# A front of eight units: priorities, early fillers, shorter conversion and loads from two queues in a 1-core attention and two-layer MoE kernel

## The chip, the cores and the metric

The kernel runs on one core of one Trainium2 chip, in fp32. The metric is the device time of one execution in microseconds. The engines are PE (matmul), DVE (vector), ACT (scalar), POOL (GpSimd) and SP (which issues DMAs).

## The reference

```
for t in range(768):                       # 4 batches x 8 heads, head_dim 40
    y[t]  = r_t . state
    Sa    = state . a_t
    state = state * w_t - Sa (x) b_t + v_t (x) k_t
x = y.transpose(0, 2, 1, 3).reshape(3072, 320)
h = max(x @ w_in, 0);  x = (h * h) @ w_out            # MoE 1, d_ff 2048
g = x @ w_gate;        out = (silu(g) * (x @ w_val)) @ w_out2   # MoE 2, d_ff 1536
```

The weights of both layers arrive as float64, the rest as float32.

## The kernel before

**The recurrence in units.** The 768 steps of all 32 heads are cut into 48 units: unit g holds 32 steps of eight heads and two such sets. Two units make a chain (I), four a block of 256 tokens, and there are 12 blocks. For each unit, e_stage loads `wakb` (w, a, k and b of the unit), takes two scans of products on DVE (L750, L758), a reciprocal (L756), the scaled AB (L754) and two scaled KB products (L762). x_stage multiplies KB with AB on PE (L779), masks the result to L on DVE (L782) and stores a part of L to `xi_d` in DRAM. inverse(w) reads `xi_d` for a window of units (in turn 2, 2, 4, 4, ...), inverts the 16x16 triangular blocks on DVE in 15 pairs of steps (L809, L812), and sends the result to DRAM and back as p1t. beside forms v (L838) and p (L845). chain does what goes from unit to unit: u (L915, L921), s (L934), the Sa tile TV (L944, L945), t (L960), ut (L963), the decayed state ST (L972). slot makes the outputs of one unit: z (L989), c (L998), the masked RC (L1001), y (L1017), yb (L1022), the state copy SX (L1032). k_stage transposes KB (L880). TV holds Sa and the loaded v, so a new chain's v loads (eight each, L705) wait for the last reader of the old one.

**Weights.** [...] The 36 pieces of MoE 1 are converted ahead of and within the first blocks; those of MoE 2 follow between the later blocks and go to DRAM.

**MoE 1.** A block of tokens is written to `xt_d` and read back as `xr`; ACT rounds it to xh (L431), DVE takes the rest as xl (L1051); xh and xl have two buffers. A block is eight pairs P: F, the in-products (L455, 16 matmuls a pair, lines of xh, xl and w1), then gh (ACT) and gl (DVE), then O, the out-products (L460). MoE 2 follows when all blocks are through.

**What sets the order.** A planner (class Plan, L72) writes the instruction order of each engine ahead of time from estimated costs: each operation has a due time (in units), an estimated cost on each engine that may do it, and what it needs; step takes the earliest engine and choose picks among what is ready by due time. On the chip each engine goes through its list in order. fill (L251) puts warm matmuls (L1188) into PE's list where it would idle between the two times of FILL_T (90 and 220 of the planner's us) and no F is ready. A DMA's landing is estimated from its bytes, and each transfer is put behind the one before.

## Time and profile before

| | us |
|---|---|
| median of the runs (lowest, highest) | 1230.94 (1227.38, 1235.12) |
| the profiled execution | 1232.03 |
| its span | 1230.0 |
| PE busy | 1105.3 |
| DVE busy | 677.2 |
| ACT busy | 528.1 |
| POOL busy | 119.3 |
| start of the first in-product (block 0) | 136.90 |
| DVE, mean of one ahead of it: PSUM memset L689, shift L420, w1l L1177 | 0.485, 0.350, 0.445 |
| DVE, the same: reciprocal, L, P, TV, ut, ST, RC, yb | 0.203, 0.417, 0.283, 0.822, 0.484, 0.540, 0.404, 0.423 |
| POOL, memset of 128x1024 | 0.95 |
| PE's one wait for a TV load, 204.4 to 406.7 | 1.6 |

The profiled execution lasted 2.0 us beyond its span and 1.1 us more than the median of the runs. Times inside the span count from its start. "Busy" is the time in which an engine has an instruction, so a difference to the length of a stretch is idle time of that engine.

### The profile page before, as it was taken

How to read it: one execution, taken by the hardware profiler on the slowest of the kernel's cores; microseconds unless marked ns; L12 is line 12 of the kernel's file. 1: busy time of each engine (PE TensorE's matmuls, PEld its weight loads, DVE VectorE, ACT ScalarE, POOL GpSimd, SP SyncE). 2: the span in 40 equal slices, each digit the busy share in tenths (PEclk: the TensorE clock that was granted, in tenths of full speed). 3: DMA queues.
4: the chain of work that ended last, by engine and by line, in shares of the span. 5: the costliest groups of instructions: out<-in, count | busy, mean ns of one | idle time of the engine just before them, and what ended most of it. 6: DMA issues, size and time to landing. Idle time of an engine off the chain costs nothing.

```text
span 1230.0 us, 44840 instructions
## 1 busy us (share of the span) xinstructions
PE 1105.3 (90%) x19570; PEld 1048.1 (85%) x19570; DVE 677.2 (55%) x1645; ACT 528.1 (43%) x1216; POOL 119.3 (10%) x146
## 2 busy tenths in 40 slices
...
GB/s 163 125 155 121 150 124 168 172 171 101 170 166 167 152 163 113 106 101 105 99 105 80 77 72 50 110 116 117 12 11 25 25 16 21 25 25 25 12 12 14
DMA packets 171093, 115.08 MB, mean 94 GB/s; under 512 B 104168, under 2 KB 147368, under 8 KB 170888
## 3 DMA queue, kind: packets, MB, share of 16 engines
...
q14 instruction: 50, 0.41, 0.1%
...
## 4 chain that ended last, share of the span: by engine, by line
PE 68%; DVE 10%; DMA 9%; issue 5%; SPq 4%; ACT 3%; POOL 1%; DVEq 0%; POOLq 0%; ACTq 0%
PE ps L455 32%; PE ps L460 20%; SPq L705 3%; PE ps L1017 2%; DMA ws<-f_moe_w_val 2%; DMA TV<-in_v_t_dram 2%; PE ps L921 2%; DMA wakb<-in_wakb_dram 2%; PE ps L998 2%; PE ps L989 1%; PE ps L934 1%; DMA room<-xt_d 1%; PE ps L779 1%; DVE qt L812 1%; PE ps L915 1%
## 5 line engine op out<-in xcount | busy, mean ns | idle before, releaser
L1361 DVE TENSOR_TENSOR gr<-ps,gr 128x512 f32<-128x512 f32 x144 | 99.5, 691 | 174.5 <-ACT gr L1358 161.0
L1099 ACT ACTIVATE ps<-ps 128x512 f32<-128x512 f32 x192 | 112.0, 584 | 118.4 <-PE ps L455 115.8
L460 PE MATMUL ps<-o1h,gh 128*128 128x320 f32 x384 | 132.9, 346 | 4.6 <-ACT gh L431 3.7
L460 PE MATMUL ps<-o1h,gl 128*128 128x320 f32 x384 | 122.8, 320 | 2.3 <-DVE gl L406 2.2
L460 PE MATMUL ps<-o1l,gh 128*128 128x320 f32 x384 | 121.3, 316 | 0.0
L455 PE MATMUL ps<-xh,w1h 128*128 128x256 f32 x384 | 119.0, 310 | 0.3 <-issue 0.3
L455 PE MATMUL ps<-xl,w1h 128*128 128x256 f32 x384 | 111.5, 290 | 3.9 <-DVE xl L1051 2.6
L455 PE MATMUL ps<-xh,w1l 128*128 128x256 f32 x384 | 111.0, 289 | 0.0
L1358 ACT ACTIVATE gr<-ps 128x512 f32<-128x512 f32 x72 | 43.2, 600 | 157.6 <-PE ps L455 156.0
L406 DVE TENSOR_TENSOR gl<-ps,gh 128x512 fp32r<-128x512 f32 x96 | 65.7, 685 | 63.0 <-ACT gh L431 62.7
L431 ACT CAST gh<-gr 128x512 fp32r<-128x512 f32 x72 | 44.7, 620 | 112.5 <-DVE gr L1361 106.5
L460 PE MATMUL ps<-o2h,gh 128*128 128x320 f32 x288 | 89.0, 309 | 2.0 <-ACT gh L431 2.0
L460 PE MATMUL ps<-o2h,gl 128*128 128x320 f32 x288 | 88.9, 309 | 0.2 <-DVE gl L1083 0.2
L460 PE MATMUL ps<-o2l,gh 128*128 128x320 f32 x288 | 88.8, 308 | 0.0
L460 PEld LDWEIGHTS ps<-o1h,gh 128*128 128x128 f32 x384 | 74.3, 194 | 8.9 <-ACT gh L431 5.3
L455 PE MATMUL ps<-xh,wgh 128*128 128x256 f32 x288 | 81.3, 282 | 0.2 <-DVE gr L1361 0.2
L455 PE MATMUL ps<-xl,wgh 128*128 128x256 f32 x288 | 80.2, 279 | 0.2 <-DVE xl L406 0.2
L455 PEld LDWEIGHTS ps<-xl,w1h 128*128 128x128 f32 x384 | 75.9, 198 | 5.0 <-DVE xl L1051 3.1
L455 PE MATMUL ps<-xh,wgl 128*128 128x256 f32 x288 | 79.9, 277 | 0.0
L455 PE MATMUL ps<-xh,wvh 128*128 128x256 f32 x288 | 79.7, 277 | 0.0
L455 PE MATMUL ps<-xl,wvh 128*128 128x256 f32 x288 | 79.7, 277 | 0.0
L455 PE MATMUL ps<-xh,wvl 128*128 128x256 f32 x288 | 79.6, 276 | 0.0
(161 smaller groups left out, 3035.3 us busy)
## 6 DMA issues: line engine op xcount, KB each, us to landing
...
```

Of the source, the lines that this page charges most:

```text
L406: nc.vector.tensor_sub(dst, full, hi.bitcast(F32))
L431: nc.scalar.copy(dst, src) if e == ACT else eng[e].tensor_copy(dst, src)
L455: nc.tensor.matmul(ps, w[:, c], x, start=(i == 0), stop=(i == len(seq_) - 1))
L460: nc.tensor.matmul(acc[t][:, :DM], g[:, half, ts], w[:, f, :], start=(f == 0 and i == 0), stop=(f == nf - 1 and i == 2),)
L705: return att({SP: slow or 0.42}, lambda e: nc.sync.dma_start(dst(), src()), r, w, due=due, dma=dma, tag="dma")
L779: nc.tensor.matmul(v[64 * p:64 * p + 64, jh, u], kb[:, s, :], ab[:, s], start=True, stop=True)
L921: nc.tensor.matmul(quad(tag)[64 * p:64 * p + 64, u, n], AB[nas[u]][:, s].rearrange("e q t -> e (q t)"), ST[u][:, s, 0:D], start=False, sto ...
L998: nc.tensor.matmul(v[64 * p:64 * p + 64, jh, u], RW[:, 4 * jh + 2 * u + p], RB[:, :, s], start=True, stop=True)
L1017: nc.tensor.matmul(v[64 * q:64 * q + D, p, s], w, x, start=not kb, stop=bool(kb))
L1099: op({ACT: 0.478}, lambda e, f=f: nc.scalar.activation(P1[b], P1[b], f), (), (("p", b),), due=due, tag="relu")
L1358: op({ACT: 0.478}, lambda e: nc.scalar.activation(two["gr"][n], two["pg"][b], AF.Sigmoid), (("pg", b),), (("gr", n),), tag="sig", **kw)
L1361: op({DVE: 0.602}, lambda e, q=q: nc.vector.tensor_mul(two["gr"][n], two[q][b], two["gr"][n]), ((q, b),), (("gr", n),), tag="u" + q, **kw)
```

## The change

Each of these is one edit; all of them act on what the planner orders or on what is computed around it.

- front(i) takes 12 units off the due times of units 0 to 3 and 6 off those of units 4 to 7. The first window is four units.
- `wakb` of units 0 to 3 comes in two pieces; eight units in place of four may use the two buffers that lie in `room`.
- The v and r loads (TV, RB, RH) of the first eight units may be issued by ACT or SP.
- BACKLOG: a load that waits for no data is issued when what is queued lasts no more than 1.2 us by the planner's estimate; the estimates of `wakb`, RB and the weight pieces are lower.
- TV and RW have two buffers. xh and xl have one in MoE 1: high_low of the next block is put in the order behind the last pair of a block; MoE 2 has two of its own.
- conv_ops: five operations. Copy with a scale of 2^-112 takes the place of Abs, the max goes, the masks follow.
- The two KB products are one of twice the elements, on DVE alone. Clears of POOL and the PSUM clears of DVE are copies from a blank tile on ACT, but for two on POOL and the blank tile's on DVE.
- FILL_T starts at 3 in place of 90. The first five weight pieces have due -9; the others come into the list behind unit 7's e_stage.

```
+        o.bulk = bool(cost) and SP in cost and not r
...
+        if o.bulk:
+            t = max(t, self.dma - BACKLOG)
...
-        t = self.free[PE]
+        t = max(self.free[PE], now - 0.02)
...
-        if t < FILL_T[0] or t > FILL_T[1] or any(o.cols for o in ok) or self.moe_cols(t + d - self.TICK, t + d) >= RAMP[2]:
+        if t < FILL_T[0] or t > FILL_T[1] or any(o.cols or t < FILL_T[2] for o in ok) or self.moe_cols(t + d - self.TICK, t + d) >= RAMP[2]:
...
+BACKLOG = 1.2
+SIDE = 4
+HEAD = 4
+AHEAD_DUE = 12.0
+W1_FIRST = 5, -9.0
...
-WIN0 = 2, 2
+WIN0 = 4,
...
-INIT_DUE = -1.0, -2.0
-HURRY = 0, 0, 0, 3
...
-FILL_T = 90.0, 220.0
+FILL_T = 3.0, 220.0, 3.0
...
-            ({ACT: t_act(n)}, lambda e: nc.scalar.activation(t.bitcast(F32), hi_f, AF.Abs), "x", "t"),
-            ({DVE: t_dve2(n), POOL: t_pool(n)}, lambda e: eng[e].tensor_scalar(
-                out=t.bitcast(F32), in0=t.bitcast(F32), scalar1=F64_TINY, scalar2=None, op0=ALU.max), "t", "t"),
+            ({ACT: t_act(n)}, lambda e: nc.scalar.activation(t.bitcast(F32), hi_f, AF.Copy, scale=F64_BASE), "x", "t"),
             ({DVE: t_dve2(n)}, lambda e: nc.vector.tensor_scalar(
-                out=t, in0=t, scalar1=3, scalar2=0x3FFFFFF8, op0=ALU.logical_shift_left, op1=ALU.bitwise_and),
+                out=t, in0=t, scalar1=3, scalar2=0x7FFFFFF8, op0=ALU.logical_shift_left, op1=ALU.bitwise_and),
                 "t", "t"),
             ({DVE: t_dve(n)}, lambda e: nc.vector.scalar_tensor_tensor(
-                out=t, in0=hi_i, scalar=-0x40000000, in1=t, op0=ALU.bitwise_and, op1=ALU.bitwise_or), "xt", "t"),
+                out=t, in0=hi_i, scalar=-0x80000000, in1=t, op0=ALU.bitwise_and, op1=ALU.bitwise_or), "xt", "t"),
...
-    xhs = ring(mp, 2, [128, 3, BT], F32R, "xh")
-    xls = ring(mp, 2, [128, 3, BT], F32R, "xl")
+    xhs = ring(mp, 1, [128, 3, BT], F32R, "xh")
+    xls = ring(mp, 1, [128, 3, BT], F32R, "xl")
...
-    TV = ap_.tile([128, 2, 8, 64], F32, name="TV")
+    TVS = ring(ap_, 2, [128, 2, 8, 64], F32, "TV")
...
-    RW = ap_.tile([EPAD, 8, 2 * C], F32, name="RW")
+    RWS = ring(ap_, 2, [EPAD, 8, 2 * C], F32, "RW")
...
+    blank = TVS[1].rearrange("p u m d -> p (u m d)")
+    nc.vector.memset(blank, 0.0)
     for b in range(8):
-        nc.vector.memset(PS[32:64, b], 0.0)
+        nc.scalar.copy(PS[32:64, b], blank[32:64, 0:512])
...
+        return -AHEAD_DUE if i < HEAD else -AHEAD_DUE / 2 if i < 2 * HEAD else 0.0
...
+    queues = {SP: nc.sync, ACT: nc.scalar}
+
+    def load(dst, src, r, w, due, dma, slow=0.0, both=False):
+        cost = {SP: slow or 0.42}
+        if both:
+            cost[ACT] = cost[SP]
+        o = att(cost, lambda e: queues[e].dma_start(dst(), src()), r, w, due=due, dma=dma, tag="dma")
+        o.bulk = not r
+        return o
 
...
-        due = g - LA + E_DUE
+        due = g - LA + E_DUE + front(g)
...
-        load(lambda: WA[wa(g)], lambda: a["wakb"][data(g)], (), (kw, ka0, ka1, kk), due - 1, 2.4)
+        if g < HEAD:
+            load(lambda: WA[wa(g)][:, 0:NWA], lambda: a["wakb"][data(g)][:, 0:NWA], (), (kw,), due - 1, 0.5)
+            load(lambda: WA[wa(g)][:, NWA:], lambda: a["wakb"][data(g)][:, NWA:], (), (ka0, ka1, kk), due - 1, 1.35)
+        else:
+            load(lambda: WA[wa(g)], lambda: a["wakb"][data(g)], (), (kw, ka0, ka1, kk), due - 1, 1.8)
...
-        for k, n in ((0, 2), (1, 1)):
-            att(two, lambda e, k=k, n=n: eng[e].tensor_mul(
-                kb[:, :, k * C:(k + 1) * C], akb[:, n], rd),
-                (kw, kk), (("KB", nk),), due=due + 0.3, tag="km", port=True)
+        att({DVE: t_dve(16 * C)}, lambda e: nc.vector.tensor_mul(
+            kb.rearrange("p s (k t) -> p k s t", k=2), akb[:, 2:0:-1], rd[:, None].to_broadcast([EPAD, 2, 8, C])),
...
-        early = FIRST if w == 0 else 0.0
+        n, due = 2 * ns * H, q0 - INV_DUE + front(q0)
...
+        if e == POOL:
+            att({POOL: t_pool(n) / 2}, lambda e: nc.gpsimd.memset(v, 0.0), (), ks, due=due, tag="init")
+        else:
+            att({ACT: t_act(n)}, lambda e: nc.scalar.copy(v, blank[0:t.shape[0], 0:n]), kblank, ks, due=due, tag="init")
...
-                         lambda p=p, jh=jh, vsrc=vsrc: vsrc[p, jh], (), (("Tv", u, p, jh),), due - 0.7, 0.12, 0.62)
+                         lambda p=p, jh=jh, vsrc=vsrc: vsrc[p, jh], (), (("Tv", b, u, p, jh),), due - 0.7, 0.12, 0.62, I < SIDE)
...
-        load(lambda: RB.rearrange("p q s t -> p (q s t)"), lambda: a["vr_e"][data(i)][:, 1], (), ("Rv",), due - 0.3, 1.2)
...
+        load(lambda: RB.rearrange("p q s t -> p (q s t)"), lambda: a["vr_e"][data(i)][:, 1], (), ("Rv",), due - 0.3, 0.9, 0.0, i < 2 * SIDE)
...
+    def high_low(blk):
+            due, kr = to_x[blk]
+            xh, xl, kx = xhs[0], xls[0], ("xh", 0)
...
+        if p == NP1 - 1 and blk + 1 < NBLK:
+            high_low(blk + 1)
...
-           kxs + [names["l"]], due=due - 1, dma=n * 1024 / 180e3, tag="dW")
+           kxs + [names["l"]], due=due - 1, dma=n * 1024 / 240e3, tag="dW")
...
-    for k, job in enumerate(w1):
-        conv(job, W1_DUE[0] + W1_DUE[1] * k / len(w1), False)
...
+            if q == 2 * HEAD - 1:
+                op(None, lambda: None, (), [("wa", x, n) for x in range(4) for n in (2, 3)] + [("xr", k) for k in range(3)]
+                   + [("o", n) for n in range(2)] + [("cx", NCX - 1), ("cl", NCX - 1)])
+                for k, job in enumerate(w1):
+                    conv(job, W1_FIRST[1] if k < W1_FIRST[0] else W1_DUE[0] + W1_DUE[1] * k / len(w1), False)
+        if I == 2:
...
+        if I == 2:
+            high_low(0)
...
+        two["xh"] = ring(sp2, 2, [128, 3, BT], F32R, "xh2")
+        two["xl"] = ring(sp2, 2, [128, 3, BT], F32R, "xl2")
```

**PE from the first chain's u.** L915 and L921 of before are L953 and L959 of after, L779 is L801 (x), L838 is L860 (v), L845 is L867 (p), L1188 is L1236 (a filler). Before:

```order
L779 MATMUL ps<-AB_148,KB_134 64x64 x8
L779 MATMUL ps<-AB_149,KB_135 64x64 x8
L915 MATMUL ps<-TV,L_123 32x40 x16
L915 MATMUL ps<-TV,L_124 32x40 x16
L921 MATMUL ps<-ST_153,AB_146 64x40 x8
L921 MATMUL ps<-ST_154,AB_147 64x40 x8
L779 MATMUL ps<-AB_150,KB_136 64x64 x8
L779 MATMUL ps<-AB_151,KB_137 64x64 x8
L779 MATMUL ps<-AB_152,KB_132 64x64 x8
L838 MATMUL ps<-p1t,L_123 32x16 x16
```

and after:

```order
L801 MATMUL ps<-AB_146,KB_132 64x64 x8
L1236 MATMUL ps<-warm 128x256 x16
L801 MATMUL ps<-AB_147,KB_133 64x64 x8
L953 MATMUL ps<-TV_157,L_121 32x40 x16
L953 MATMUL ps<-TV_157,L_122 32x40 x16
L959 MATMUL ps<-ST_151,AB_144 64x40 x8
L959 MATMUL ps<-ST_152,AB_145 64x40 x8
L1236 MATMUL ps<-warm 128x256 x90
L801 MATMUL ps<-AB_148,KB_134 64x64 x8
L1236 MATMUL ps<-warm 128x256 x2
L860 MATMUL ps<-p1t,L_121 32x16 x16
L860 MATMUL ps<-p1t,L_122 32x16 x16
```

Behind the first chain's u stand 90 fillers, then the x product of one more unit, and only then v, which waits for the first inverse; before, three x products stand there and no filler.

**SP between the first `wakb` loads and the first read of `xi`.** `pt_d` is a table of zeros in DRAM, cx a weight piece, `xi_d` the stored part of L. Before:

```order
L705 DMA RH<-in_r_e_dram 40x512 x2
L705 DMA TV<-in_v_t_dram 32x4x40 x8
L705 DMA wakb_166<-in_wakb_dram 104x1040
L705 DMA xi_d_60<-L_123 32x256 x2
L705 DMA wakb_167<-in_wakb_dram 104x1040
L705 DMA xi_d_60<-L_124 32x256 x2
L705 DMA xi_d_61<-L_125 32x256 x2
L705 DMA xi_d_61<-L_126 32x256 x2
L1147 DMA room<-in_moe_w_out_dram 128x320
L1147 DMA cx_116<-in_moe_w_out_dram 128x320
L1147 DMA cx_117<-in_moe_w_in_dram 128x256
L705 DMA xi<-xi_d_60 32x16x16 x2
```

and after:

```order
L722 DMA xi_d_60<-L_121 32x256 x2
L722 DMA TV_157<-in_v_t_dram 32x4x40 x4
L722 DMA xi_d_60<-L_122 32x256 x2
L722 DMA RB<-in_vr_e_dram 104x512
L722 DMA xi_d_60<-L_123 32x256 x2
L722 DMA RH<-in_r_e_dram 40x512
L722 DMA TV_158<-in_v_t_dram 32x4x40 x4
L722 DMA xi_d_60<-L_124 32x256 x2
L1195 DMA cx_114<-in_moe_w_in_dram 128x256
L1195 DMA cx_115<-in_moe_w_in_dram 128x256
L1195 DMA cx_116<-in_moe_w_in_dram 128x1x256
L722 DMA xi<-xi_d_60 64x16x16 x2
```

The stores to `xi_d` of four units in place of two stand ahead of the read of `xi`; eight v loads stand between them, the other eight of the first two chains are in ACT's list, and no further `wakb` load stands ahead of the read.

**ACT around the first xh.** L416 and L417 (after: L422, L423) open a conversion, L713 (after: L732) are sums of squares for a range test at the end. Before:

```order
L431 CAST o1h<-ct_120 128x320
L416 ACTIVATE room<-room 128x256
L417 ACTIVATE ct_122<-room 128x256
L431 COPY KT_157<-ps 128x320
L431 CAST w1h_99<-ct_121 128x256
L713 ACTIVATE sq,stat<-DT_142 104x256
L431 CAST w1h_100<-ct_122 128x256
L431 CAST xh_111<-room 128x768
L713 ACTIVATE sq,stat<-wakb_166 104x256
```

and after:

```order
L422 ACTIVATE room<-room 128x320
L423 ACTIVATE ct_120<-room 128x320
L435 CAST o1h<-ct_120 128x320
L732 ACTIVATE sq,stat<-wakb_167 104x256
L435 CAST w1h_99<-ct_118 128x256
L732 ACTIVATE sq,stat<-DT_138 104x256
L435 CAST w1h_100<-ct_119 128x256
L435 CAST o1h<-ct_117 128x320
L435 CAST xh_111<-room 128x768
L435 COPY vt<-ps 128x8x16
```

The xh of block 0 stands behind the same kinds of work in both; of the weight pieces, 22 are loaded ahead of the first pair before, and 13 after.

## Rows read from the trace of the kernel before

**Rows 1.** The first part of the page: busy us, share of the span, instructions

```profile
PE 1105.3 (90%) x19570; PEld 1048.1 (85%) x19570; DVE 677.2 (55%) x1645; ACT 528.1 (43%) x1216; POOL 119.3 (10%) x146
```

**Rows 2.** Windows, cut at block starts: length, PE, PEld, DVE, ACT, POOL, granted clock, DMA share

```profile
0.00:97.00 97.00, 44.70 (x1088) 38.16 (x1089) 83.26 (x251) 38.91 (x114) 29.10 (x44) 1.00 0.55 143
0.00:136.90 136.90, 74.17 (x1945) 64.38 (x1946) 108.35 (x309) 53.45 (x157) 35.83 (x52) 0.96 0.54 141
136.90:204.40 67.50, 55.33 (x1301) 50.69 (x1300) 50.40 (x133) 42.58 (x108) 21.16 (x24) 0.90 0.55 143
204.40:272.20 67.80, 59.81 (x1310) 55.36 (x1309) 45.04 (x126) 37.16 (x88) 14.46 (x16) 0.93 0.67 184
272.20:346.00 73.80, 63.27 (x1586) 57.88 (x1586) 48.63 (x132) 38.15 (x95) 13.49 (x14) 0.96 0.48 126
346.00:406.70 60.70, 56.53 (x1249) 52.80 (x1249) 39.37 (x109) 33.38 (x81) 9.73 (x11) 0.90 0.60 161
```

**Rows 3.** Timeline around block 0's first in-product: start, us, engine, line, operation

```profile
133.88 0.83 ACT L431 CAST xh<-room 128x768 fp32r<-128x768 f32 x1
...
134.74 0.96 DVE L1051 SCALAR_TENSOR_TENSOR xl<-room,xh 128x768 fp32r<-128x768 f32 x1 [0.31 <-ACT xh L431]
...
136.90 0.41 PE L455 MATMUL ps<-xh,w1h 128*128 128x256 f32 x1
```

**Rows 4.** PE's waits, 0 to 136.9: us in total, times, longest us

```profile
PE ps L779 <- DVE KB L762: 36.8, 7, 16.0
```

**Rows 5.** DVE's groups, 0 to 136.9: busy us, mean ns, idle time ahead

```profile
L809 DVE TENSOR_TENSOR tmp<-qt,xi 64x15 f32<-64x15 f32 (+15 forms) x45 | 10.8, 240 | 2.1 <-DMA xi<-xi_d 1.2
L762 DVE TENSOR_TENSOR KB<-wakb 104x256 f32<-104x256 f32 x22 | 10.2, 477 | 0.2
L754 DVE TENSOR_TENSOR AB<-wakb,DT 40x256 f32<-40x256 f32 x20 | 10.1, 507 | 0.2
L812 DVE TENSOR_TENSOR qt<-qt,tmp 64x15 f32<-64x15 f32 (+15 forms) x45 | 9.6, 213 | 1.1
...
L423 DVE SCALAR_TENSOR_TENSOR ct<-cx,ct 128x256 int32<-128x256 int32 (+1 forms) x15 | 7.1, 477 | 0.0
...
L418 DVE TENSOR_SCALAR ct<-ct 128x256 f32<-128x256 f32 (+1 forms) x17 | 5.5, 326 | 0.4 <-ACT ct L417 0.4
...
L1177 DVE TENSOR_TENSOR o1l<-ct,o1h 128x320 fp32r<-128x320 f32 x7 | 4.5, 650 | 0.3 <-ACT o1h L431 0.2
```

**Rows 6.** Timeline of SP's queue

```profile
13.76 9.69 SPq L705 DMA_DIRECT2D TV<-in_v_t_dram  x8
```

**Rows 7.** The chain of waits, pieces up to block 0: start, us, what

```profile
23.57 4.41 DMA wakb<-in_wakb_dram
...
138.97 2.92 DMA xi<-xi_d
```

**Rows 8.** Timeline of PE: two x products

```profile
52.55 1.12 PE L779 MATMUL ps<-AB,KB 104*64 104x64 f32 x16 [16.02 <-DVE KB L762]
...
107.33 0.69 PE L779 MATMUL ps<-AB,KB 104*64 104x64 f32 x16
```

**Rows 9.** Timeline: POOL and DVE side by side, at two places

```profile
7.16 0.36 POOL L902 MEMSET SX<- 104x320 f32 x1
7.16 0.71 DVE L750 TENSOR_TENSOR_SCAN DT<-wakb,c 104x264 f32<-104x264 f32 x1 [1.46 <-DMA wakb<-in_wakb_dram]
...
39.25 0.91 POOL L425 TENSOR_TENSOR ct<-ct,room 128x320 int32<-128x320 int32 x1 [1.82 <-DVE tmp L809]
39.35 0.83 DVE L812 TENSOR_TENSOR qt<-qt,tmp 64x15 f32<-64x15 f32 x1
```

**Rows 10.** PE's waits, 204.4 to 406.7

```profile
PE ps L845 <- ACT ct L417: 3.5, 1, 3.5
...
PE ps L455 <- DVE xl L1051: 2.6, 2, 2.2
```

**Rows 11.** The chain of waits of the whole span, one out-product

```profile
850.86 3.52 PE ps L460 x24
```

115 lines of the change are left out of this document (62 added, 53 removed).

## The prediction

> **What bounds the kernel now.** The page's first part comes first: PE is busy for 1105.3 of 1230.0 us [rows 1], so the time is PE's work plus what PE loses, and the question is where it loses. The table of windows, cut at the first F matmul of each token block (the end of the front, 136.90, is the first L455 in the timeline [rows 3]), shows where: in the front, 0 to 136.9, PE is busy for 74.17 us, fillers included, so 62.7 are idle; the next four blocks lose 12.2, 8.0, 10.5 and 4.2; what lies behind runs at 90% or more and holds PE work that the change leaves alone [rows 2]. So the change is worth what it shortens the front, less the work that it pushes out of it, plus what it does to the next four blocks.
>
> What sets the front? DVE is busy for 108.35 of its 136.9 us, for 83.26 of the first 97 [rows 2], and the chain of waits to 138.29 is mostly DVE rows with pieces of SP and DMA between. PE's own waits there are one line in the main: its x products wait for DVE's KB 36.8 us in 7 waits [rows 4], which is PE standing in order behind a late DVE. So I count DVE operations.
>
> **The front, part by part.** The count is of DVE instructions ahead of the first xl in each order; each goes by its mean in the front [rows 5].
> - conv_ops without the max step, and fewer jobs ahead of block 0: max 17 to 0 (17 x 0.326 = 5.5), shift 20 to 12 (8 x 0.350 = 2.8), L423 20 to 12 (8 x 0.477 = 3.8), the w1l/o1l subtractions 15 to 8 (7 x 0.54, between 445 and 650, = 3.8). Sum 15.9.
> - The inverse of one four-unit window in place of two of two units: 90 operations to 60. They cost 240 and 213 ns, so 30 x 0.227 = 6.8. A tile of 128 rows in place of 64 costs the same here, since the elements of a row stay.
> - Fewer units ahead of block 0: scans 26 to 22 (4 x 0.71 = 2.8), AB 24 to 16 (8 x 0.507 = 4.1), and one each or so of L, P, TV, ut, ST, RC, yb and reciprocals (5.1).
> - KB: 26 products of 0.477 (the four of `room` 0.402) are 11.7 us; 11 merged ones of twice the elements take their place. No row has one. Bounds: 0.69, on the line between the 256 elements of w1l (0.445) and the 768 of xl (0.96 [rows 3]), and 0.95, twice 0.477. I take 0.75, since xl, the only row with more elements, is as wide as the merged product in partitions and lies far under three times 0.477: 8.3 us, 3.4 less.
> - Clears: eight PSUM memsets of 0.485 leave DVE for ACT; one memset of 128x1024 comes (the same shape cost POOL 0.95), 2.9 less. ACT takes some 16 copies, about 8 us, in its empty start (38.91 busy of 97 [rows 2]), at no price while DVE waits for its first wakb, until 7.16 [rows 9]; up to 2 if the split load lets the first scan start earlier and a clear stands before it.
>
> Sum 40.9: DVE's work falls from 108.35 to 67.4 us. The loads of v and r: eight TV issues hold SP for 9.69 us from 13.76 [rows 6], while DVE waits for the `wakb` behind them (23.57, 4.41 on the chain [rows 7]). In the order of after some of them stand on ACT, so two queues share the 1.2 us a piece.
>
> DVE's idle time in the front was 136.9 - 108.35 = 28.55. I keep two thirds, 19 us, as the waits for the first wakb (7) stay, and the waits from TV issues fall. A new wait comes: the first inverse needs the L of all four units, and the store of the fourth stands on SP behind four TV issues (4 x 1.21 = 4.8); then `xi` has to land (2.92 [rows 7]): 8 us in which DVE has little ready, since the conversion is ordered behind. So 27 idle, and block 0 starts at 67.4 + 27 = 94 us, bounds 78 (idle 11, as if the new wait is covered and SP no longer shows) to 105 (idle 38: the new wait doubles). That is 43 us earlier. But PE has done 12 groups fewer by then: at 0.69 each, the x row at 107.33 [rows 8], 8.3 us that come later. Net 34.6.
>
> **Early fillers.** Fillers grow from 80 to 308 matmuls, 244 of them ahead of block 0, in idle time of PE. They raise the clock if anything: 16 x products took 1.12 us at 52.55 behind a 16 us gap and 0.69 at 107.33 [rows 8]. Yet the table's granted clock reads 1.00, the 2.4 GHz level, over 0 to 97 [rows 2], and the front hangs on DVE; a group on the chain saves 0.4, and with some eight on it, 3 us. I book nothing, as a filler ahead of a late group delays it by about as much as it saves.
>
> **The port.** At 39.25 a POOL addition of 0.91 us stands beside a DVE step of 0.83 that takes 0.213 in the mean, while a POOL memset at 7.16 leaves the scan beside it at 0.71, its usual time [rows 5, 9]. So clears that go to ACT give DVE nothing beyond its own eight. Eight L425 additions fewer ahead of block 0 (they fall with the jobs) may free 8 x 0.6 = 5 us; I book nothing, since a mean of 213 over 45 steps says that such meetings are few.
>
> **Blocks 0 to 1.** The work that left the front comes here. DVE's count between the first and second xl is 20.2 us higher (no max, but 11 more shifts, 10 more L423, 6 more wl, four scans, and so on by the same means): 50.40 + 20.2 = 70.6. How full DVE can run decides: in the front's first 97 us it was busy 0.86 of the time (83.26/97), here 0.75 (50.40/67.5), in the next three 0.65 to 0.66 [rows 2]. I take 0.86, since here, as in the front and unlike in the stage before, there would be more DVE work than PE work: 82 us against 67.5, 14.5 more, which holds the 13 us of PE work (17 groups and a u) that moved in. Net loss 1.5; at 0.75 it would be 94 us, 12 worse, at 0.65 109, 27 worse. The sum stands at 33.
>
> **Blocks 1 to 4.** Before, PE was idle for 12.2 + 8.0 + 10.5 + 4.2 = 35 us in blocks 0 to 3 [rows 2]; its waits from 204 to 407 are many small ones, by name L845 for a conversion's ct 3.5 and F for xl 2.6 [rows 10], for a TV load 1.6. Two Sa buffers take the TV wait away, a max less per job shortens the ct wait, fewer conversions wait on DVE: 8 of 35 us, bounds 0 and 20. Behind 406.7 nothing is moved that PE waits for: two `xh` in MoE2 as before.
>
> **The single xh/xl buffer** adds a wait: xh of the next block may not be written before the last F of this one, and xl behind it holds up the next F: 0.83 + 0.96 [rows 3]. PE then has 12 L460 matmuls (half of 24 in 3.52 [rows 11], 1.76) and one group each of c, x and z (three at 0.69 [rows 8]): 3.8 us that cover 1.8 and two hand-overs. I book zero; what is queued in order behind them on ACT and DVE is conversions, due later.
>
> **Sum.** 34.6 - 1.5 + 8 = 41 off 1232.0, the profiled execution's own time, is 1191; it lies 1.1 above the median of the runs, so 1190. From the bounds: 78 in the front with 20 in the blocks gives 1162; 105 and no gain in the blocks, 1209; the rivals reach to 1222.
>
> **Rivals.**
> 1. *Conversion takes the gain back* (0.18). ACT and DVE run in order; jobs that were ahead of block 0 now interleave with e-stage and F's gh/gl. For it: DVE's share was 0.65 in three of four blocks [rows 2]. Against: there PE was the busier. The stage is 27 longer: 1232 - 41 + 27 - 1 = 1217.
> 2. *DMA binds* (0.11). Block 0 needs 13.4 MB by the order of after; at 141 GB/s [rows 2] that is 95 us, already the forecast. If the rate stays there because the transfers and not the issues limit it, and the short queue (BACKLOG) lets the engines run dry for a tenth of the time, block 0 comes 11 us later, and so does block 1 by as much again (12.8 MB): 1232 - 41 + 23 - 1 = 1213. Against: DMA's share is 0.55 there and rose to 0.67 at 184 GB/s in a later block [rows 2], so there is room. The Trainium skill speaks for this rival ("DMA: Bandwidth & Descriptors", section "Issuing engines are not separate DMA queues"): transfers that another engine starts run on the same 16 DMA engines, and a second issuer saves no more than the time of the issue. The 9.69 us that eight issues take are such time, so the trace leaves the rule standing and the gain too.
> 3. *Slower* (0.07): the one xh/xl. Each of 11 block starts waits with ACT and DVE in order: if a gh, a conversion pair and an e-stage piece stand ahead of xh, 5 us are lost beyond the cover, 55 in all: 1232 - 41 + 55 - 1 = 1245. It decides from (41 + 12)/11 = 4.8 us each. Against: blocks started before with xl as the last to come [rows 3, 10] and lost 2.6 in two waits.
> 4. *More* (0.12): block 0 at 80, blocks 1 to 4 losing 15 in place of 35: 1164.
> That the change doesn't do what it says is open only for fillers and port, which I booked at nothing.
>
> **How the numbers follow.** The forecast, 1190, has 0.52; the rivals the rest. The range of 1160 to 1222 holds all but rival 3 and some of rival 1's tail. A measurement of this kernel tells 1% from no change: 12.3 us, so faster is under 1218.6 and slower over 1243. Faster: 0.52 + 0.11 + 0.12 + 0.10 of rival 1 = 0.85; same 0.08, from rival 1's; slower 0.07.
>
> **What would show it.** In the profile of after: first L459 at 94 (78 to 105); DVE about 67 us busy ahead of it; second block's first F 82 us behind; merged KB at 0.75; PE's longest wait in the front the one for the first inverse, at 25 to 35 us; no wait for TV in blocks 1 to 4; waits of F for xl under 1 us a block. I am wrong if block 0 starts past 105, if block 0 takes 100 or more, or if xl waits come to 5 a block.

## The result, and the profile after

The kernel after takes 1224.39 us in the median of 20 runs (1211.89 to 1237.83), the kernel before 1234.38 (1224.03 to 1241.7): a ratio of 0.9911, interval 0.9885 to 0.9936. The ratio goes by the executions in the faster of the chip's two states, 18 of the 20 of after. It is faster, by 0.9% or 11 us, where 41 were forecast; 1190 and the range up to 1222 are both missed on the high side. By the forecast's own line of 12.3 us for telling a change this counts as the same, to which it gave 0.08; the interval excludes no change all the same. Before itself measures 3.4 us more here than the 1230.94 under the forecast: on that base 0.9911 is 1220, inside the range at its upper end. So the range is missed by less than two measurements of before differ, but of the gain only a quarter came.

The profiled execution of after lasted 1218.24 us (span 1216.3), 6 less than its median, so the sums below, against the 1232.03 of before, come to 13.8 and not to 11.

The first part of the page of after, to be read against [rows 1]:

```profile
PE 1128.3 (93%) x19798; PEld 1072.6 (88%) x19798; DVE 643.4 (53%) x1492; ACT 538.4 (44%) x1238; POOL 106.3 (9%) x127
```

PE's span that is not busy falls from 124.7 to 88.0 us, yet PE is busy for 23.0 us more. The windows of after, cut at the first F of blocks 0, 1, 4 and 11 (columns as in [rows 2]):

```profile
0.00:111.00 111.00, 72.99 (x1724) 65.53 (x1725) 73.09 (x192) 49.94 (x134) 20.33 (x30) 0.86 0.52 133
111.00:214.00 103.00, 83.78 (x2031) 76.45 (x2029) 70.21 (x173) 62.13 (x161) 36.41 (x38) 0.85 0.54 149
214.00:388.40 174.40, 166.81 (x4033) 154.63 (x4029) 115.19 (x305) 95.65 (x234) 22.89 (x26) 0.96 0.57 149
388.40:760.80 372.40, 361.69 (x8555) 336.01 (x8553) 199.48 (x529) 192.06 (x442) 25.88 (x32) 0.99 0.45 116
760.80:1216.30 455.50, 443.04 (x3468) 439.95 (x3466) 185.48 (x296) 138.59 (x269) 0.74 (x1) 0.99 0.13 35
```

And before, from its block 0 on, cut at its first F of blocks 1 (205.4; [rows 2] cut it at 204.4), 4 and 11:

```profile
136.90:205.40 68.50, 56.33 (x1318) 51.41 (x1317) 50.99 (x134) 42.58 (x108) 21.16 (x24) 0.90 0.55 143
205.40:406.70 201.30, 178.61 (x4128) 165.32 (x4126) 132.45 (x363) 108.69 (x264) 37.67 (x40) 0.93 0.58 156
406.70:784.90 378.20, 365.12 (x8720) 339.19 (x8721) 200.57 (x544) 185.10 (x419) 23.86 (x29) 0.99 0.41 102
784.90:1230.00 445.10, 431.08 (x3467) 427.84 (x3465) 184.80 (x296) 138.27 (x269) 0.74 (x1) 0.99 0.13 35
```

Fillers alone take 15.7 us before, all in the front; after, PE's fillers in the front and in block 0:

```profile
0.00:111.00 111.00, 40.48 (x244) 0.86 0.52 133
111.00:214.00 103.00, 10.65 (x66) 0.85 0.54 149
```

| stage, us | before | after | measured | forecast | PE's own work | idle and fillers |
|---|---|---|---|---|---|---|
| front | 136.9 | 111.0 | -25.9 | -43 | -26.0 | +0.1 |
| block 0 | 68.5 | 103.0 | +34.5 | +14.5 | +16.8 | +17.7 |
| blocks 1 to 3 | 201.3 | 174.4 | -26.9 | -12.7 | -11.8 | -15.1 |
| blocks 4 to 10 | 378.2 | 372.4 | -5.8 | 0 | -3.4 | -2.4 |
| block 11 and MoE 2 | 445.1 | 455.5 | +10.4 | 0 | +12.0 | -1.6 |

The forecast column follows from the sum on record: what it moves into block 0, and the part of that which comes from later blocks, stands with the stage in which it is saved or paid. The last two columns split the measured change: PE's own work is its busy time without fillers, the rest of a stage is idle time and fillers. The first three stages moved in the direction given; the two booked at nothing gain 5.8 and lose 10.4.

**The front.** DVE's groups in the front of after (busy us, mean ns, idle time ahead):

```profile
L831 DVE TENSOR_TENSOR tmp<-qt,xi 128x15 f32<-128x15 f32 (+7 forms) x30 | 6.7, 225 | 6.6 <-DMA xi<-xi_d 5.8
...
L773 DVE TENSOR_TENSOR_SCAN DT<-wakb,c 104x264 f32<-104x264 f32 x7 | 5.7, 810 | 2.2 <-DMA wakb<-in_wakb_dram 2.2
...
L784 DVE TENSOR_TENSOR KB<-wakb 104x512 f32<-104x512 f32 x7 | 5.4, 773 | 0.0
...
L424 DVE TENSOR_SCALAR ct<-ct 128x256 int32<-128x256 int32 (+1 forms) x12 | 4.9, 404 | 10.7 <-ACT ct L423 10.5
...
L784 DVE TENSOR_TENSOR KB<-room 104x512 f32<-104x512 f32 x4 | 2.7, 669 | 0.0
```

The merged KB takes 0.773 and 0.669 us, 0.735 in the mean, so 0.75 was a good guess, and a step of the inverse costs 225 ns on 128 rows where it cost 240 on 64 [rows 5]. Single rows moved (this scan from 0.71 [rows 9] to 0.810, the shift from 0.350 to 0.404, the inverse's steps down), but the durations of DVE's operations ahead of block 0 add up to 121.4 us before and 80.3 after, 41.1 less, as counted (40.9). DVE's busy time falls by 35.3 only, to 73.1 us and not 67.4: in the record the spans of neighbouring operations overlap, by 13 us in all before and 7 after, and the forecast took durations off a busy time. And DVE idles 37.9 us and not 27, of which 10.5 are for the ct that ACT makes (L423) and 5.8 for `xi`. Both lie in one place, as DVE's timeline shows (start, duration, engine, line; the idle time ahead in brackets), and SP's under it:

```profile
19.11 0.42 DVE L804 TENSOR_TENSOR L<-ps,mask 128x256 f32<-128x256 f32 x1 [1.32 <-PE ps L801]
28.43 0.29 DVE L424 TENSOR_SCALAR ct<-ct 128x256 int32<-128x256 int32 x1 [8.89 <-ACT ct L423]
...
35.00 0.17 DVE L831 TENSOR_TENSOR tmp<-qt,xi 128x15 f32<-128x15 f32 x1 [5.82 <-DMA xi<-xi_d]
```

```profile
19.77 3.03 SPq L722 DMA_DIRECT2D TV<-in_v_t_dram  x4
22.89 0.99 SPq L722 DMA_DIRECT2D xi_d<-L  x2
23.93 2.56 SPq L1195 DMA_DIRECT2D cx<-in_moe_w_in_dram  x3
26.60 4.05 SPq L722 DMA_DIRECT2D xi<-xi_d  x2
```

The last L of the first window ends at 19.53. Its stores stand behind four TV issues, as foreseen (19.77, 3.03 long); then SP issues three weight pieces for 2.56 us, and then the reads of `xi`, 4.05 us long. The inverse begins at 35.00: in 15.5 us DVE does two conversion steps. The term was 8.

**PE's waits.** Two rows, one of the front, one of 214 to 388 (in total, times, longest):

```profile
PE ps L801 <- DVE KB L784: 17.1, 2, 15.9
...
PE ps L459 <- DVE xl L1097: 0.2, 1, 0.2
```

The 36.8 us of [rows 4] fell to 17.1, and the single xh/xl costs nothing: F waits for xl 0.2 us in three blocks, as booked. No wait names a TV load there. PE's longest wait in the front, 15.9 us, ends at 48.35 and is for a KB; the forecast had expected one for the first inverse at 25 to 35.

### The profile page after: what moved, and what is told of

It reads as the page before. It is cut to its first block, busy times and chain, and to the rows that moved or that the text cites. A ratio compares the mean times of both kernels' runs of the same rounds, so it can differ in the third digit from the quotient of the medians.

```text
span 1216.3 us, 45103 instructions
## 1 busy us (share of the span) xinstructions
PE 1128.3 (93%) x19798; PEld 1072.6 (88%) x19798; DVE 643.4 (53%) x1492; ACT 538.4 (44%) x1238; POOL 106.3 (9%) x127
## 3 DMA queue, kind: packets, MB, share of 16 engines
q1 hardware_dynamic: 168462, 110.58, 34.6%
## 4 chain that ended last, share of the span: by engine, by line
PE 70%; DMA 5%; SPq 3%; DVE 3%; issue 2%; ACT 2%; DVEq 0%; ACTq 0%
PE ps L459 33%; PE ps L464 22%; SPq L722 3%; PE ps L1056 2%; DMA ws<-f_moe_w_val 2%; PE ps L1037 2%; PE ps L1028 1%; PE ps L959 1%; PE ps L998 1%; PE ps L1071 1%; DMA P<-pt_d 1%; PE ps L801 1%; PE ps L972 1%; PE ps L867 1%; PE ps L953 1%
## 5 line engine op out<-in xcount | busy, mean ns | idle before, releaser
L459 PE MATMUL ps<-xh,w1h 128*128 128x256 f32 x384 | 116.0, 302 | 0.2 <-issue 0.2
L435 ACT CAST gh<-gr 128x512 fp32r<-128x512 f32 x72 | 44.6, 620 | 112.0 <-DVE gr L1410 106.2
L412 DVE TENSOR_TENSOR gl<-ps,gh 128x512 fp32r<-128x512 f32 x96 | 65.5, 682 | 43.6 <-ACT gh L435 43.4
L464 PEld LDWEIGHTS ps<-o1h,gl 128*128 128x128 f32 x384 | 74.6, 194 | 5.3 <-DVE gl L412 5.3
```

Source lines behind the costliest of these rows:

```text
L412: nc.vector.tensor_sub(dst, full, hi.bitcast(F32))
L435: nc.scalar.copy(dst, src) if e == ACT else eng[e].tensor_copy(dst, src)
L459: nc.tensor.matmul(ps, w[:, c], x, start=(i == 0), stop=(i == len(seq_) - 1))
L464: nc.tensor.matmul(acc[t][:, :DM], g[:, half, ts], w[:, f, :], start=(f == 0 and i == 0), stop=(f == nf - 1 and i == 2),)
```

## Experiments

**What had to be told apart.** The forecast had one frame: the time is PE's work plus its idle time, so the kernel gains what the front loses. Four readings of the miss stood against each other: that the conversion of MoE 1's weights, pushed out of the front, filled block 0; that early fillers stand in PE's way; that MoE 2, whose x tiles got another place, works more slowly; and that the planned order scatters so much that small terms mean nothing. Words in capitals in the expectations are names of such readings. All ratios are to the kernel before; in the table are also the starts of three blocks (their first F) and the length from block 11 on, from each run's profile. Before has 205.4, 784.9 and 445.1 for the last three columns.

| run | ratio | interval | block 0 | block 1 | block 11 | last stage |
|---|---|---|---|---|---|---|
| after | 0.9911 | 0.9885-0.9936 | 111.0 | 214.0 | 760.8 | 455.5 |
| after_again | 0.9898 | 0.9842-0.9953 | 113.5 | 215.9 | 766.9 | 455.5 |
| jit_x | 0.992 | 0.9879-0.996 | 111.0 | 209.3 | 769.0 | 457.0 |
| jit_add | 0.9913 | 0.9876-0.9951 | 110.9 | 208.5 | 773.6 | 457.5 |
| x2_high | 0.98 | 0.9765-0.9835 | 110.0 | 212.5 | 770.3 | 447.9 |
| late_fill | 0.9835 | 0.9794-0.9876 | 113.7 | 199.7 | 756.3 | 457.3 |
| x2_late | 0.9768 | 0.9721-0.9816 | 116.5 | 198.7 | 752.5 | 445.8 |
| split_late | 0.9787 | 0.9712-0.9863 | 114.1 | 198.7 | 752.5 | 451.2 |
| no_prio | 0.9915 | 0.9876-0.9954 | 124.4 | 188.2 | 771.1 | 456.6 |
| max_back | 0.9926 | 0.9884-0.9967 | 116.5 | 221.9 | 774.2 | 455.2 |
| w1_earlier | 0.9988 | 0.9951-1.0024 | 108.5 | 197.9 | 775.8 | 455.0 |
| xi_gate | 0.9951 | 0.9917-0.9985 | 117.7 | 208.8 | 773.9 | 455.6 |
| one_queue | 1.0008 | 0.9979-1.0038 | 110.7 | 197.4 | 775.2 | 456.1 |
| long_queue | 1.0006 | 0.9966-1.0046 | 114.1 | 199.2 | 786.1 | 456.2 |
| x2l_one | 0.9864 | 0.9807-0.9921 | 110.7 | 213.7 | 767.8 | 447.8 |
| x2l_long | 0.9974 | 0.994-1.0008 | 129.7 | 194.9 | 784.8 | 447.0 |
| x2l_short | 1.0385 | 1.031-1.0461 | 103.8 | 196.6 | 824.0 | 458.3 |

Two more ran only once: w1_cheap (1209.51 us) and x2_mixed (1208.18).

### The place of MoE 2's x tiles: x2_high, x2_mixed, split_late

After takes MoE 2's two xh and two xl from the ring at the low end of the partition. x2_high lays the odd blocks' tiles into the pool of the out-weights at the high end, and lets the even ones use MoE 1's. MoE 2's weights, which lie behind that ring, move back down with it; the order of DVE's and ACT's operations is that of after.

```
-        two["xh"] = ring(sp2, 2, [128, 3, BT], F32R, "xh2")
-        two["xl"] = ring(sp2, 2, [128, 3, BT], F32R, "xl2")
...
+        two["xh"] = [xhs[0]] + ring(wo2, 1, [128, 3, BT], F32R, "xh2")
+        two["xl"] = [xls[0]] + ring(wo2, 1, [128, 3, BT], F32R, "xl2")
```

> One edit to the changed kernel: MoE 2's two xh and two xl no longer lie beside MoE 2's input weights but at the far end of the partition (one pair is MoE 1's tile, the other a new one behind o2), as far from the weights as in the kernel before. The order up to block 11 stays. Theory PLACE: in the changed kernel MoE 2's in-products start 120 ns apart where they were 113 ns apart before, because the moved operand now lies in the same part of SBUF as the weights; here the spacing is 113 to 114 again, the last stage (block 11's first in-product to the end) takes 445 in place of 455.5 us, the run about 11 us less than the changed kernel (near 1213). Rival RUN: the 120 is a state of that run or follows from something else in the program (the order, the new weight offsets); then the spacing stays at 119 to 120 and the time at about 1224.

The step of the blocks of MoE 2 is read from the timeline of DVE's xl (L406 before, L412 after), here two successive blocks of before, of after and of x2_high:

```profile
1013.71 1.02 DVE L406 TENSOR_TENSOR xl<-ps,xh 128x384 fp32r<-128x384 f32 x2
...
1046.90 1.02 DVE L406 TENSOR_TENSOR xl<-ps,xh 128x384 fp32r<-128x384 f32 x2
```

```profile
1028.08 1.02 DVE L412 TENSOR_TENSOR xl<-ps,xh 128x384 fp32r<-128x384 f32 x2
...
1062.26 1.02 DVE L412 TENSOR_TENSOR xl<-ps,xh 128x384 fp32r<-128x384 f32 x2
```

```profile
1034.65 1.02 DVE L412 TENSOR_TENSOR xl<-ps,xh 128x384 fp32r<-128x384 f32 x2
...
1067.98 1.02 DVE L412 TENSOR_TENSOR xl<-ps,xh 128x384 fp32r<-128x384 f32 x2
```

The step is 33.19, 34.18 and 33.33 us. And inside a block, by PE's timeline, successive in-products of before and of after:

```profile
999.73 0.28 PE L455 MATMUL ps<-xh,wvl 128*128 128x256 f32 x1
999.85 0.28 PE L455 MATMUL ps<-xh,wvhl 128*128 128x256 f32 x1
999.96 0.28 PE L455 MATMUL ps<-xl,wvhl 128*128 128x256 f32 x1
```

```profile
1000.06 0.28 PE L459 MATMUL ps<-xh,wvh 128*128 128x256 f32 x1
1000.18 0.28 PE L459 MATMUL ps<-xl,wvh 128*128 128x256 f32 x1
1000.30 0.28 PE L459 MATMUL ps<-xh,wvl 128*128 128x256 f32 x1
```

Every product lasts 0.28, but they start 113 ns apart before and 120 after: same shapes, same clock (0.99 in both windows), no wait between. In x2_high the last stage is 447.9 in place of 455.5 and the ratio 0.98 against 0.9911 (0.9898 in the second measurement): the place costs about 1%. The last stage shows 7.6 us of it, 0.6%; the intervals leave room for that.

x2_mixed keeps the xl of odd blocks at the low end, beside the weights, and moves the rest as x2_high does.

> As the run with MoE 2's x far away, but the xl of odd blocks stays beside the weights, all else far. PLACE, and the operand is what counts: in-products that read xh, and those of even blocks that read xl, start 113 ns apart; those of odd blocks that read xl 120, all within one execution. If the offset of the weights counts and not that of x, all are equal. If one near tile disturbs the others, odd blocks are slow throughout.

Its last stage is 450.4, between the two; the products of xh and of xl are 118 and 120 ns apart in its odd blocks, 113 in its even ones: the third reading, odd blocks slow throughout, and with the weights in one place, so that the place of x matters by itself. split_late is x2_late (below) with MoE 1's x and g tiles in a pool of their own at the start of the partition:

```
+    xg = xgs.enter_context(tc.tile_pool(name="xg", bufs=1, side="left"))
...
-    xhs = ring(mp, 1, [128, 3, BT], F32R, "xh")
+    xhs = ring(xg, 1, [128, 3, BT], F32R, "xh")
```

> The kernel with late fillers and MoE 2's x far from its weights, and one edit more: MoE 1's xh, xl and both layers' gh, gl lie at the start of the partition (17,696 to 32,032) in place of its end, so that every product of both layers has its two operands in different parts. Theory PARTS (a pair of operands of which one lies below about 110,000 and the other above is quick): MoE 1's in-products go from a median of 119 to 120 ns to 113 to 114, the out-products of both layers from 147 to about 140; time 15 to 25 us under the kernel without this edit (1201), near 1180. Rival ONE SIDE (only x behind, weights ahead is quick): in-products of MoE 1 stay at 119, the out-products at 147, time unchanged within 4. Rival PHASE: MoE 1's spacing comes from the other engines' traffic; in-products stay and only MoE 2's out-products move.

MoE 2's products are then 118 apart, and those of MoE 1, 119 to 120 in before and after, 114 to 117. So the place is shown to count, but the rule that was expected of it fell, and no other was found. Nor is the place all. x2_high, x2_late and x2l_short (below) have the same tiles in the same places. Their even blocks run at 113 to 114 ns; the odd ones run at 118 throughout in x2l_short, but in the other two at 118 in block 1 and at 114 from block 3 on.

### Early fillers: late_fill, x2_late

```
-FILL_T = 3.0, 220.0, 3.0
+FILL_T = 90.0, 220.0, 3.0
```

> One number of the changed kernel: fillers from 90 of the planner's us on, as in the kernel before, in place of 3. Theory CLOCK: what the change won is in PE's own work (attention matmuls took 279.0 us in place of 293.6, MoE 1's 8.8 us less), since fillers had warmed PE; without them the attention matmuls ahead of block 0 take 45 to 50 us in place of 33.7 and the time is 4 to 10 us longer than the changed kernel. Rival COVER: the front is set by DVE, SP and the first inverse, so a slower PE there changes the first in-product by under 3 us and the time by under 4. Rival LOAD: fillers stand in front of late groups and cost; then it is 3 to 8 us faster.

The fillers of after in the first 400 us (busy us, mean ns, idle ahead), then the page's PE line and the fillers of late_fill:

```profile
L1236 PE MATMUL ps<-warm 128*128 128x256 f32 x308 | 51.1, 316 | 16.7 <-DVE L L804 6.9 <-ACT warm L435 6.6 <-issue 1.7
```

```profile
PE 1111.1 (92%) x19570; PEld 1056.9 (87%) x19570; DVE 643.8 (53%) x1502; ACT 536.1 (44%) x1239; POOL 96.6 (8%) x116
...
L1236 PE MATMUL ps<-warm 128*128 128x256 f32 x80 | 16.3, 368 | 0.5 <-DVE L L804 0.5
```

After spends 51.1 us on 308 fillers, late_fill 16.3 on 80. What is left of PE's busy time is 1077.2 in after (1082.7 in after_again, the same kernel) and 1094.8 in late_fill, so early fillers save PE 12 to 18 us of its own work. The timeline shows how: x products of after with a window of its granted clock, and an x product of late_fill.

```profile
10.07 0.69 PE L801 MATMUL ps<-AB,KB 104*64 104x64 f32 x16
...
48.35 1.12 PE L801 MATMUL ps<-AB,KB 104*64 104x64 f32 x16 [15.94 <-DVE KB L784]
...
48.00:54.00 6.00, 3.23 (x84) 2.79 (x85) 5.89 (x12) 1.84 (x7) 2.24 (x2) 0.50 0.29 86
```

```profile
13.53 1.12 PE L801 MATMUL ps<-AB,KB 104*64 104x64 f32 x16 [2.90 <-DVE c L779]
```

Behind fillers the product takes 0.69, behind none 1.12, and 1.12 too in after once PE has stood idle from 32.4 to 48.35; the granted clock there is 0.50, the 1.2 GHz level. But idle time and fillers together fall from 139.1 us in after to 118.7 in late_fill, by 20.4, more than the 12 to 18. late_fill is faster than after, 0.9835 (up to 0.9876) to 0.9911 (from 0.9885). The edit also gives DVE and ACT another order, so the fillers' own part of the 0.8% is not shown. Both edits together:

> Two edits to the changed kernel that each helped alone: MoE 2's x tiles far from its weights, and fillers from 90 on. If the two gains are of different places (the last stage; block 0) they add: about 10 and 8 us off, near 1205, 0.975 of the kernel before. If the late fillers' gain was scatter between chips, it is 0.98, as the far x alone.

0.9768, the best kernel of this study, 1200.92 us: 2.3% under before and 1.4% under after. On that base leaving out the early fillers gives 0.3% (0.98 to 0.9768), which its interval doesn't tell from nothing.

### The conversion: w1_cheap, max_back, w1_earlier

In after conv_ops makes float32 bits of a float64 weight piece by five operations, two on ACT (L422, L423), two on DVE (L424, L427) and one on POOL (L429); then come a high part (ACT, L435) and a low part (DVE, L1225). For MoE 1, w1_cheap leaves out four of the five, all but the scaled copy of the upper words (L423); the high and low parts are still taken.

```
-            for cost, fn, rd, wr in conv_ops(x, t, n):
+            for cost, fn, rd, wr in conv_ops(x, t, n)[0 if store else 1:6 if store else 2]:
```

> The changed kernel, where the conversion of MoE 1's weights leaves out four of its five operations (only the scaled copy of the upper words stays, so the weights are not the reference's); loads, high and low parts and every product stay. Theory CONV: block 0 lasts until the 36 pieces are converted, at about 4.4 us a piece in both kernels (the last addition on POOL starts at about 210 in both), so the front that was won is given back there. Then block 1's first in-product comes at 160 to 190 in place of 214 and the time falls by 12 to 30 us. Rival ORDER: attention's chain and the DMA queue set block 0 (p1t, RB and SP's issues are what PE is seen to wait for); then block 1 still starts after 205 and the time falls by under 6 us.

Its windows from block 0 to block 4:

```profile
113.60:179.50 65.90, 56.75 (x1294) 52.63 (x1287) 41.49 (x102) 40.94 (x103) 8.58 (x11) 0.89 0.61 161
179.50:382.20 202.70, 188.94 (x4729) 173.49 (x4729) 119.50 (x312) 98.73 (x246) 22.56 (x26) 0.93 0.55 138
```

Block 0 takes 65.9 us in place of 103.0, its DVE works 41.49 in place of 70.21: the conversion does fill block 0. But PE does 1072 matmuls of the recurrence in this shorter block 0 and not 1752, blocks 1 to 3 then take 202.7 in place of 174.4, and by the two profiled executions (1209.51 and 1218.24) the kernel ends some 9 us earlier, by the ratios (0.980 for its one execution) some 13: of 37 us that block 0 gains, a quarter to a third is left. max_back puts Abs and the max back:

> The changed kernel with the six-step conversion of the kernel before (Abs, a max, masks of 30 bits). Per piece 0.33 us of DVE or 0.5 to 0.7 of POOL come back, 36 pieces of MoE 1 by block 1. Theory CONV: block 0 is bound by the rate of pieces, so block 1 starts 5 to 12 us later; of that, as when four of five steps were left out (block 1 at 179.5, total 9 less), only a third reaches the end: +2 to +5. Rival: nothing at the end, under 2.

Block 1 starts 8 us later than in after; the ratio, 0.9926 to 0.9911, shows nothing. w1_earlier lets 16 pieces in place of five have due -9:

```
-W1_FIRST = 5, -9.0
+W1_FIRST = 16, -9.0
```

> One number of the changed kernel: the first 16 weight pieces in place of five have the early due time, so conversion starts earlier against units 0 to 7. Theory CONV: block 1 starts at 200 or earlier; by what the run without four conversion steps showed, up to a third of that reaches the end (-3 to -6). Rival SUM: what the end shows is PE's work and the time in which PE has none, over all blocks; a different cut between front and block 0 moves block starts by 10 us and the end by under 3 (as the run without priorities: first in-product 13 later, block 1 26 earlier, time the same).

Block 1 starts 16 us earlier and the kernel ends 0.8% later, against every expectation.

### Front and chain: no_prio, xi_gate

```
-AHEAD_DUE = 12.0
+AHEAD_DUE = 0.0
```

> One number of the changed kernel: the due times of the first eight units get nothing taken off (12 and 6 units before). Theory PRIO: the short front comes from them; the first in-product then comes after 120 and the time rises by 5 or more. Rival WORK: the front is shorter because there is less in it (one inverse window, five operations a piece, 13 pieces in place of 22) and the order is set by what is ready; then first in-product within 5 of 111, time within 4 of the changed kernel.

```profile
0.00:124.40 124.40, 93.88 (x2022) 86.08 (x2023) 83.62 (x219) 58.36 (x155) 23.90 (x30) 0.79 0.56 144
124.40:188.20 63.80, 56.33 (x1114) 51.46 (x1112) 52.34 (x137) 46.23 (x122) 21.90 (x25) 0.95 0.62 166
188.20:387.70 199.50, 184.68 (x4652) 171.02 (x4645) 120.63 (x326) 99.94 (x249) 20.82 (x24) 0.92 0.55 141
```

The windows of no_prio show it: without the priorities the front is 13.4 us longer, block 0 39 shorter and blocks 1 to 3 25 longer, and the time is the same. xi_gate goes at the 15.5 us wait of the first inverse: four weight pieces and the `wakb` of units 4 to 7 stand behind the reads of `xi` (their loads depend on them).

```
-                 [...], (kx[r],), due - 1, 0.8, 0.7)
+                 [...], (kx[r],) + ((("gate", r),) if w == 0 else ()), due - 1, 0.8, 0.7)
```

> The changed kernel with an order among loads: the first four weight pieces and the wakb of units 4 to 7 stand behind the two reads of xi of the first window in SP's list (three pieces stood ahead). Theory WAIT: the first inverse starts at 29 to 31 in place of 35.0, the first in-product comes 3 to 6 us earlier, and since front and block 0 are paid for by PE's idle time the end comes 2 to 5 earlier. Rival CHAIN: the inverse starts earlier, but the weight pieces come as much later and DVE's e-stages for units 4 to 7 wait for their wakb in its place; first in-product and end within 3.

DVE's first step of the inverse, and SP's last stores and its reads of `xi`:

```profile
30.50 0.18 DVE L831 TENSOR_TENSOR tmp<-qt,xi 128x15 f32<-128x15 f32 x1 [9.80 <-DMA xi<-xi_d]
...
23.06 0.99 SPq L722 DMA_DIRECT2D xi_d<-L  x2
26.80 1.38 SPq L722 DMA_DIRECT2D xi<-xi_d  x2
```

The inverse begins 4.5 us earlier, the first F 6.7 later, the end no earlier. SP issues the reads of `xi` at 26.80 here and at 26.60 in after: the weight pieces ahead of them do not delay the start of the issue. Without them the issue is 2.7 us shorter and the landing 2 us. As the weights and the `wakb` loads come later by the same edit, it shows that an earlier inverse bought in this way gains nothing; that the front's end doesn't hang on the inverse is not shown.

### Queues: one_queue, long_queue, x2l_one, x2l_long, x2l_short

one_queue gives the v and r loads of the first units back to SP (SIDE = 0); long_queue takes the limit off what may be queued (BACKLOG = 1e6).

> One number of the changed kernel: the loads of v and r of the first eight units all go through SP again (23 issues leave ACT). Theory ISSUE: a v issue costs 0.6 to 0.7 us on either engine, and SP's list ahead of the first inverse gets four more of them; the first inverse starts 2 to 4 us later and the first in-product 3 to 8 later, time +2 to +6. Rival SPENT: on ACT they take the place of copies and sums in an engine that is as much in order as SP, so the front moves by under 3 and the time by under 3 either way.

> One number of the changed kernel: bulk loads are issued as soon as the order allows, with no limit on what is queued (BACKLOG a million in place of 1.2). Theory QUEUE: with the short queue small reads (xi, p1t, RB) no longer stand behind weight pieces; without it the first inverse comes later (first xi wait over 6 us), block 0 is longer, time +4 to +10. Rival FREE: the buffers (four for weight pieces) bound the queue anyway; within 4 of the changed kernel.

Each loses the whole gain: 1.0008 and 1.0006. With one queue block 0 starts as in after (110.7 to 111.0), so the price is not paid where it was expected. By PE's sums over the span one_queue has 13.6 us more of idle time and fillers than after and 1.5 more of PE's own work, long_queue 11.8 and 14.2. The x2l kernels do the same to x2_late, and x2l_short halves the limit to 0.6:

> The best kernel so far (late fillers, MoE 2's x far from its weights; 0.977 of the kernel before) with all loads of v and r on SP. If a second issuing queue is worth 1% by itself, as it was in the changed kernel, this is 0.985 to 0.989. If that 1% was the luck of an order, 0.974 to 0.982.

> The best kernel so far with no limit on queued bulk loads. If the short queue is worth 1% by itself: 0.985 to 0.990 of the kernel before, the wait for the first xi or p1t longer than with it. If that was the luck of an order, 0.974 to 0.982.

> The best kernel so far (0.977 of the kernel before) with the limit on queued bulk loads at 0.6 in place of 1.2. If a shorter queue goes on paying, 0.968 to 0.974. If 1.2 is short enough, 0.974 to 0.980. If issues now come too late to keep the transfers going, 0.982 or more.

1.0% (the intervals just touch) and 2.1% over x2_late, so both prices appear on a second base too, the second larger than expected. At 0.6 it is 6.3% (the windows are cut up to 1 us behind the first F):

```profile
0.00:104.80 104.80, 47.57 (x1370) 42.13 (x1370) 69.63 (x181) 46.80 (x124) 14.77 (x25) 0.93 0.51 130
104.80:196.60 91.80, 75.05 (x1512) 68.46 (x1512) 63.66 (x158) 54.32 (x139) 23.95 (x27) 0.89 0.48 131
196.60:396.00 199.40, 178.08 (x4053) 162.46 (x4046) 113.58 (x295) 94.11 (x228) 14.18 (x16) 0.93 0.47 120
396.00:825.00 429.00, 393.28 (x9237) 361.62 (x9237) 230.76 (x589) 203.00 (x478) 27.14 (x31) 0.94 0.45 117
```

Block 0 starts earlier than in any other kernel here, and from block 4 to 11 it takes 429.0 us in place of 371.9. Up to block 4 DMA's share is lower than in x2_late (0.51, 0.48 and 0.47 to 0.55, 0.60 and 0.58, in the windows below), as if the short queue let the engines run dry; behind it, where most of the time is lost, 0.45 is no lower than in after (0.45).

### How much the planned order scatters: after_again, jit_x, jit_add

jit_x raises the planner's cost of an x product from 0.47 to 0.48, jit_add lowers its rate for the weight pieces from 240 to 238, so that only the order changes.

> The changed kernel as it is, once more, as the yardstick for the other runs on this chip and for how far one profile stands for the kernel. Expected: 0.99 of the kernel before, first in-product at 110 to 112, block 1 at 212 to 216, PE's time outside useful work (idle and fillers) 130 to 145 us.

> The changed kernel with a number that means nothing: the planner's cost of an x product 0.48 in place of 0.47, which puts some 3150 of PE's 7280 rows in another place. If the planner's orders are alike in worth, the time stays within 0.3% of the changed kernel (0.988 to 0.994 of the kernel before). Rival SCATTER: any newly planned order moves the time by up to 1%, and what single edits to the due times cost or gave (1.000 with one queue, 1.001 with a long queue, 0.999 with earlier weights, 0.9915 without priorities) says little of the part; then this run lies outside 0.987 to 0.995.

> The same with another such number: the planner's rate for weight pieces 238 in place of 240 thousand. Alike: 0.988 to 0.994 of the kernel before. SCATTER: outside.

0.9898, 0.992 and 0.9913: the two chance reorderings move the ratio by up to 0.1%, each known to 0.4%. Two are few, so that differences of 0.8% and more above are those of the edits is likely, and surest where they come on two bases. The starts of blocks move by up to 13 us with a reordering (block 11), and by 6 with none (after_again), so a stage of one profile is no measure of such an edit.

## Why the prediction was wrong

**The step that failed.** "So the change is worth what it shortens the front, less the work that it pushes out of it, plus what it does to the next four blocks." The forecast's 41 us are all time that PE stands idle: 34.6 in the front, 1.5 lost in block 0, 8 won in the blocks. Measured, the front's idle time and fillers are what they were (+0.1): it is 25.9 us shorter because 26.0 us of PE's own work left it (1864 matmuls of the recurrence before, 1480 after, part of them faster behind fillers), where the forecast took 12 groups, 8.3 us, off. Block 0 then loses 17.7, blocks 1 to 3 win 15.1. Over the whole span PE's idle time and fillers were 140.4 us before (124.7 and 15.7) and are 139.1 after: the change filled gaps with fillers, and gained in PE's own work (1089.6 to 1077.2), which was booked at nothing and a part of which MoE 2 took back. As a sum the frame holds; as a way to find the gain it failed, since the stages are not independent. no_prio, xi_gate, w1_earlier and x2l_short move the start of block 0 or 1 by 5 to 26 us with no gain at the end, or a loss. Two of its three signs of being wrong came: block 0 starts past 105 and takes over 100.

**"So I count DVE operations".** The chain of waits to 138.29 is not mostly DVE by time: some 48 us of its first 70 are, but of the 68 behind them DVE has 9, DMA 23, PE 22 and SP 7. The count covered half of the front.

**"So 27 idle, and block 0 starts at 67.4 + 27 = 94".** The operations were counted rightly; the 67.4 became 73.1 because durations that overlap were taken off a busy time. The new wait was 15.5 and not 8 (37.9 idle in all): 111.0. The stores behind the four TV issues took about the 4.8 foreseen. What was left out is 2.7 us until SP starts the reads of `xi` (in xi_gate too, with nothing issued between) and 4.05 for their issue, and the landing took over 4 and not 2.92.

**"I take 0.86".** DVE's work in block 0 is 70.2, as worked out (70.6), but DVE is busy for 0.68 of that stage, which is 21 us longer than forecast; it is rival 1's mechanism, shown by w1_cheap, and nearly its size (27). Of the 34.5 us that block 0 grows PE's own work is 16.8, fillers 10.6 and idle time 7.0. What no rival had is that much of this came back: blocks 1 to 3 are 27 us shorter and not 13, 15.1 of it idle time. Recurrence done ahead is little of that (3356 of its matmuls there, 3424 before). So the conversion holds 9 to 13 us by a single execution, and not the whole. The idle time of blocks 0 to 3 fell from 35 to 27, the 8 that were booked, but by luck: block 0 idles 7.0 more and the others 15.1 less.

**"Behind 406.7 nothing is moved that PE waits for: two `xh` in MoE2 as before".** True of waits, and wrong by 10.4 us: PE itself works more slowly there, and x2_high, with the tiles in another place, has most of it back (7.6). With about 1% this is the largest single loss at the end.

**"I book nothing" for early fillers.** They do save PE time (12 to 18 us), more than the 3 that I allowed, and they stand in its way for more: late_fill is 0.8% faster than after, x2_late 0.3%, within the error, faster than x2_high. The forecast read the granted clock of 1.00 in the front of before as the 2.4 GHz level; but the ten x products there up to 87.19 all take 1.12 us, what one takes in after where the clock reads 0.50.

**Two queues and the short queue.** Kept: each is worth 1% or more, on two bases. Rival 2, in which the short queue lets the engines run dry, had the wrong sign at 1.2; at 0.6 its sign is right, but the shares show dry engines only up to block 4. The 23 loads that ACT issues in after take it 13.5 us, and on SP a TV issue takes 0.76 (3.03 for four), so 14 to 17 us are taken off SP, and 12 show at the end. The Trainium skill ("DMA: Bandwidth & Descriptors", section "Issuing engines are not separate DMA queues") has it that a second issuer saves no more than the time of the issue. The trace leaves that rule standing.

**Right:** the merged KB (0.735), the single xh/xl at no price and no wait for TV, so that rival 3 has nothing to act on. **Not told:** the max step and the clears were booked at 5.5 and 2.9 us of DVE's front; of the max, max_back finds nothing at the end, and clears and port were not tried alone. Nor were the window of four, the merged KB, the second TV and the split `wakb`.

With the two losses taken out some 70% of the forecast gain is there. The windows of x2_late:

```profile
0.00:116.50 116.50, 57.52 (x1584) 51.06 (x1584) 78.35 (x204) 53.99 (x145) 18.18 (x28) 0.93 0.55 139
116.50:198.70 82.20, 70.84 (x1597) 63.23 (x1590) 61.05 (x153) 52.90 (x137) 27.01 (x29) 0.89 0.60 159
198.70:380.60 181.90, 173.66 (x4382) 161.64 (x4381) 118.12 (x317) 99.47 (x248) 26.44 (x29) 0.96 0.58 150
```

Its front of 116.5 is no shorter than that of after, yet block 0 (82.2) makes up for it, and block 4 starts at 380.6 where after stood at 388.4 and before at 406.7. That 82.2 is the forecast's number is luck: DVE is busy for 61.05 us there, 0.74 of the time, and not for 70.6 at 0.86. The ratio of 0.9768 is 1206 us of 1234.4, where the forecast asked for 0.967.

**Open:** why a place in the partition changes the spacing of products, by which rule, and what else does; through which loads the two queue settings act behind block 0; and what the front's second half hangs on.
